# Attention loads in one queue, value products and transposes in other slots: a local-attention and gated-network kernel

## The chip, the cores and the metric

The kernel runs on one core of one Trainium2 chip. The metric is the device time of one execution in microseconds (us). The engines of a core are TensorE (PE in the profile: matrix products, with PEld for loading their stationary operand), VectorE (DVE), ScalarE (ACT), GpSimd (POOL) and SyncE (SP). Each engine works through its own list of instructions in order. DMAs (transfers between device memory and on-chip memory) are started from the lists of SyncE, ScalarE or GpSimd, and 16 DMA engines carry them out.

## What is computed

Local attention over chunks, then two gated networks, all in float32:

```python
# q, k, v: (4, 8, 768, 64); mem_k, mem_v: (4, 8, 8, 64)
for c in range(24):                                  # chunks of 32 queries
    l_start, r_end = max(0, 32*c - 16), min(768, 32*c + 40)
    k_full = concat([mem_k, k[:, :, l_start:r_end]])  # 8 memory keys + up to 56 keys
    v_full = concat([mem_v, v[:, :, l_start:r_end]])
    s = (q_c @ k_full.T) / 8
    a = exp(s - max(s));  a = a / (sum(a) + 1e-9)
    out_c = a @ v_full
x = out, as (3072 tokens, 512)
h = ((x @ w1) * (x @ w2)) @ w3;  x = h @ w_out        # 512 -> 1024 -> 512
y = ((x @ w_a) * (x @ w_b)) @ w_out2                  # 512 -> 1536 -> 512
```

## The kernel before, in words

The work is written out by hand in a set order; every engine's list follows the order of the program text.

**First stage.** The product of `w3` and `w_out` is formed on TensorE: two halves of 32 products of 128x512 outputs (in float32 each is two records `wps` in the trace), whose order is the list `order` of pairs (k, m). The weights arrive as raw blocks, `raw` (twelve of 1 MB: `w3a` x8, `w3b` x4; then sixteen of 0.5 MB of `w1`/`w2`), on SyncE's queue. `w_tick` moves a pipeline of four steps on by one: subtract the low part of one block, cast the high part of the next, sum the bits of the next on VectorE (`w_sum`, L359 and L360), scale the next on ScalarE (`w_scale`, L354 and L355), and then issue the loads whose buffers came free (`w_load`, L339; four buffers for the 1 MB blocks, three for the 0.5 MB ones). Three ticks run ahead of the first product, and 16 more among them.

**Attention.** The 3072 tokens are worked in 16 units of 192 tokens (u = 0 to 15). A unit loads its keys (`a_k`, two DMAs of 256 KB), queries (`a_q`, two of 192 KB) and values (`a_v`, twelve of 112 and 16 KB, as rows of 512 bytes); each of the three has one buffer, so the load of one unit waits until the unit before it has read that buffer. The steps of a unit are: `a_keys` (VectorE copies the key windows, L148, L149), `a_scores` (96 small matmuls `sc`), `a_max` (VectorE), four `a_exp` (ScalarE, four exponentials L195 each), two `a_norm` (sum and reciprocal on VectorE, the product on GpSimd, L212), `a_trans` (eight transposes `pt` on TensorE, L223), `a_pt` (ScalarE copies them out, L229), `a_pv` (96 small matmuls `xp` with the values) and `a_x` (the result is split into a high part on ScalarE and a low part on VectorE). `xp` and `pt` share one PSUM buffer.

**Slots.** `STAGES` gives each step its slot relative to 9u, and `attn_slot` runs all steps of one slot in the order of the table. In the first stage `attn_slot` is called after certain products; at its end the slots up to `NEED[0]` are done. In the second stage (the first network over six tiles of 512 tokens, `ti` = 0 to 5) the function `between`, called after each twelve large matmuls (`psA`, `psB`) or part of `psY`, does a `w_tick` while there are `w1`/`w2` blocks, later a step of converting the second network's weights (`cw`), and then as many slots as bring the count on evenly to `NEED[ti + 1]`: 27 or 18 slots in 22 calls. The third stage, from 621 us on, has no attention.

**Queues.** Loads of units 0 to 2 (`u < UA`) are issued from GpSimd, except the keys and queries of unit 0, which are issued from ScalarE after the third tick; from unit 3 on all are on SyncE. Weights, results and intermediate stores are on SyncE as well.

Of the kernel before, what the change touches and what calls it, by code (L numbers as in the profile page):

```python
# [14 lines left out]
B, H, S, D = 4, 8, 768, 64  # L15
NMEM = 8
CHUNK, LEFT, RIGHT = 32, 16, 8
GQ = 96
# [5 lines left out]
TT = 512  # L24
NT1 = B * S // TT
NU = B * NG * 2
NE = 2
NA = B * NG // NE
UA = -(-TT // (NE * GQ))
# [16 lines left out]
def tile_attention_moe(  # L46
# [16 lines left out]
    nc = tc.nc  # L63
# [25 lines left out]
    def mm(o, l, r, first, last):  # L89
        nc.tensor.matmul(o, lhsT=l, rhs=r, start=first, stop=last)  # L90
# [8 lines left out]
    def split_lo(lo, src, hi):  # L99
        nc.vector.tensor_tensor(lo, src, hi.bitcast(F32), ALU.subtract)  # L100

    def queue_of(u):
        return nc.gpsimd if u < UA else nc.sync

    def rows(r):
        return slice(D * r, D * r + D)

    def a_k(u, eng=None):
        if u >= NA:
            return  # L110
        k = ks[u] = att.tile([P, NE * 2, 2 * KW], F32, tag="kraw", bufs=1, name="kraw")
        for r in range(2):
            src = kt[2 * NE * u : 2 * NE * u + 2 * NE, 0:D, 2 * r : 2 * r + 2, :]
            (eng or queue_of(u)).dma_start(out=k[rows(r)], in_=src.rearrange("a d h k -> d a (h k)"))

    def a_q(u, eng=None):
        if u >= NA:
            return
        q = qs[u] = att.tile([P, NE * 2, 2 * GQ], F32, tag="q", bufs=1, name="q")
        for r in range(2):  # L120
            src = qt[2 * NE * u : 2 * NE * u + 2 * NE, :, 2 * r : 2 * r + 2, :]
            (eng or queue_of(u)).dma_start(out=q[rows(r)], in_=src.rearrange("a d h q -> d a (h q)"))

    def a_v(u):
        if u >= NA:
            return
        v = vs[u] = att.tile([P, NE * 2, NC, 2 * D], F32, tag="v", bufs=1, name="v")
        for r in range(2):
            src = vw[2 * NE * u : 2 * NE * u + 2 * NE, :, 2 * D * r : 2 * D * r + 2 * D]
            src = src.rearrange("a k d -> k a d")  # L130
            for c in range(NC):
                k0 = NMEM + CHUNK * c
                eng = queue_of(u)
                eng.dma_start(out=v[D * r : D * r + NMEM, :, c, :], in_=src[0:NMEM])  # L134
                eng.dma_start(  # L135
                    out=v[D * r + NMEM : D * r + D, :, c, :], in_=src[k0 : k0 + KEYS - NMEM]
                )

    def a_keys(u):
        if u >= NA:  # L140
            return
        k = ks.pop(u).rearrange("p a (h k) -> p (a h) k", h=2)
        kw = kws[u] = att.tile([P, NH, NC, KEYS], F32, tag="kw", bufs=1, name="kw")
        p, a, e = k.ap
        win = bass.AP(
            k.tensor, k.offset + NMEM * e[0], [p, a, [CHUNK * e[0], NC], [e[0], KEYS - NMEM]]
        )
        nc.vector.tensor_copy(kw[:, :, :, NMEM:], win)  # L148
        nc.vector.tensor_copy(  # L149
            kw[:, :, :, 0:NMEM], k[:, :, None, 0:NMEM].to_broadcast([P, NH, NC, NMEM])  # L150
        )
# [38 lines left out]
    def a_exp(i):  # L190
        def stage_of(u):
            sc, t, mx, sm = soft[u]
            for a in range(2 * i, 2 * i + 2):
                for r in range(2):
                    nc.scalar.activation(  # L195
                        t[:, a, r, :],
                        sc[:, r, a, :],
                        AF.Exp,
                        bias=mx[:, r, a : a + 1],
                        scale=SCALE,  # L200
                        accum_out=sm[:, a, r : r + 1],
                    )

        return stage_of

    def a_norm(e):
        def stage_of(u):
            t, mx, sm = soft[u][1:]
            t, sm = t[:, 4 * e : 4 * e + 4], sm[:, 4 * e : 4 * e + 4]
            nc.vector.tensor_scalar_add(sm, sm, 1e-9)  # L210
            nc.vector.reciprocal(sm, sm)
            nc.gpsimd.tensor_tensor(  # L212
                t, t, sm[:, :, :, None].to_broadcast([GQ, 4, 2, KEYS]), ALU.mult
            )

        return stage_of
# [33 lines left out]
    def a_x(u):  # L250
# [17 lines left out]

    NS_U = 9
    STAGES = (  # L270
        (10, a_x),
        (8, a_pt),
        (9, a_pv),
        (7, a_trans),
        (1, a_max),
        (2, a_exp(0)),
        (3, a_exp(1)),
        (3, a_exp(2)),
        (4, a_exp(3)),
        (4, a_norm(0)),  # L280
        (5, a_norm(1)),
        (0, a_scores),
        (1, lambda u: a_q(u + 1)),
        (5, lambda u: a_keys(u + 1)),
        (6, lambda u: a_k(u + 2)),
        (10, lambda u: a_v(u + 1)),
    )
    todo = {}
# [1 line left out]
        for j, (s, stage_of) in enumerate(STAGES):  # L290
            todo.setdefault(NS_U * u + s, []).append((j, u, stage_of))
    acount = [0]
    NEED = [NS_U * (-(-TT * (i + 1) // (NE * GQ)) - 1) + 11 for i in range(NT1)]

    def attn_slot(n=1):
        for _ in range(n):
            s = acount[0]
            if s >= NEED[-1]:
                return
            acount[0] += 1  # L300
            for _, u, stage_of in sorted(todo.get(s, []), key=lambda x: x[:2]):
                stage_of(u)
# [83 lines left out]
    def w_tick():  # L386

        if len(pipe[2]):
            i, a, ax, (d, f, w, hi, lo) = pipe[2].pop(0)
            nc.vector.tensor_tensor(lo, a, hi.bitcast(F32), ALU.subtract)  # L390
            live["dec"][ax] -= 1
            d[f] = w
        if pipe[1]:
            i, a, ax = pipe[1].pop(0)
            t = w_place(*plan[i][:3])
            nc.scalar.activation(t[3], a, AF.Copy)
            pipe[2].append((i, a, ax, t))
        if len(pipe[0]):
            i, r, tag = pipe[0].pop(0)
            a, ax = w_sum(i, r)  # L400
            live[tag][int(tag == "raw2")] -= 1
            if ax is not None:
                pipe[1].append((i, a, ax))
        if wraw:
            i, r, tag = wraw.pop(0)
            for (r1,) in pieces_of(i, r):
                w_scale(r1)
            pipe[0].append((i, r, tag))
        while w_load():
            pass  # L410
# [122 lines left out]
    w_load()  # L533
    for i in range(3):
        w_tick()
    a_k(0, nc.scalar)
    a_q(0, nc.scalar)

    def w_evict(half, m):
        w = wsm[4 * half + m] = w_new(wpool, "wo")  # L540
        nc.scalar.activation(w[:, 0, :], banks[m], AF.Copy)
        nc.vector.tensor_tensor(w[:, 1, :], banks[m], w[:, 0, :].bitcast(F32), ALU.subtract)
# [3 lines left out]
    for half in range(2):  # L546
        banks = [psd.tile([P, 512], F32, tag="d", name="wps") for _ in range(4)]
        for k, m in order:
            mm(
                banks[m],  # L550
                w3k[8 * half + k].bitcast(F32)[:, P * m : P * m + P],
                wo_f[k].bitcast(F32),
                k == 0,
                k == 7,
            )
            if k < 6 and m % 2 == 0 or k == 6:
                continue

            if half == 0:
                if k == 2 and m == 3:  # L560
                    a_keys(0)
                    a_k(1)
                    a_v(0)
                if m == 1 or k == 7 and m == 3:
                    w_tick()
                attn_slot(int(k > 2))
            else:
                if k < 6:
                    if m == 3:
                        w_tick()  # L570
                    attn_slot(1 + (m == 3 and k < 5))
                else:
                    if m % 2 == 1:
                        w_tick()
                    if m < 2:
                        attn_slot()
            if k == 7 and m > 0:
                w_evict(half, m - 1)
        w_evict(half, 3)
# [36 lines left out]
    def between():  # L616
# [10 lines left out]
        if ti < NT1 - 1:  # L627
            b = nstep[0] - NB * ti
            n = (NEED[ti + 1] - NEED[ti]) * b // (NB - 2)
            attn_slot(min(NEED[ti] + n, NEED[ti + 1]) - acount[0])  # L630

# [49 lines left out]
    for ti in range(NT1):  # L681
        last = ti == NT1 - 1
        gs = {}
        attn_slot(NEED[ti] - acount[0])
        if last:
# [320 lines left out]
```

## Time and profile before

| | |
|---|---|
| median of 3 runs | 1165.67 us (1165.38 to 1169.14) |
| the profiled execution | 1166.5 us; span 1164.7 us from its first to its last instruction, 1.8 us around it |
| TensorE busy | 1072.4 us (92% of the span) |
| VectorE, ScalarE, GpSimd busy | 462.9, 440.0, 264.8 us |
| mean granted clock of TensorE | 0.963 of 2.4 GHz (0.50 is 1.2 GHz) |
| first large matmul of the second stage | at 154.36 us |

A large matmul (128x512) is the unit in which TensorE works; a product of the first stage is two of them, a block of `psA` or `psB` twelve. A time in brackets behind an instruction is how long its engine stood idle before it, and the name behind the arrow is what ended that; "issue" means that the profile shows nothing the engine waited for.

### The profile page before, as it was taken

Reading aid. Unit: us, or ns where it says so; the run is one execution under the profiler, and the core shown is the slowest. Engines: PE = TensorE matmul, PEld = TensorE weight load, DVE = VectorE, ACT = ScalarE, POOL = GpSimd, SP = SyncE. Lnnn points to the kernel's source line nnn. Section 1 sums busy time; section 2 is a strip of 40 time slices with the busy share of each in tenths; the row PEclk is TensorE's granted clock in tenths of the full one; section 3 lists DMA queues with packets and bytes.
Section 4 is the critical chain, followed back from the end, with each engine's and each line's share of the span. In section 5 each row is a group of like instructions: output and inputs, shape, how many; then the busy total and the mean of one; then the engine's idle time right before and its main releaser. Section 6 shows DMA issues by size and latency. Waiting matters only on the chain.

```text
span 1164.7 us, 18629 instructions
## 1 busy us (share of the span) xinstructions
PE 1072.4 (92%) x7442; PEld 857.8 (74%) x7442; DVE 462.9 (40%) x763; ACT 440.0 (38%) x1153; POOL 264.8 (23%) x272
## 2 busy tenths in 40 slices
PE   6553489899999999999999999999999999999998
PEld 2222267787788778788888888888888888888887
DVE  3431267324445355253566334344222325222220
ACT  6332366444355365344444333333222223222220
POOL 0223212202122123031121322311232220323210
PEclk9777799899999999999999999999999999999999
DMA  9712544464345454632654554552444352534400
GB/s 338 218 54 66 131 132 124 131 186 132 110 150 154 147 157 138 184 108 102 221 193 157 199 207 171 208 174 74 160 151 166 127 199 73 189 128 143 174 37 36
DMA packets 80411, 173.22 MB, mean 149 GB/s; under 512 B 8317, under 2 KB 42621, under 8 KB 74437
## 3 DMA queue, kind: packets, MB, share of 16 engines
q1 hardware_dynamic: 66644, 100.82, 27.4%
q0 software_dynamic: 12384, 70.27, 16.9%
q8 instruction: 58, 0.95, 0.3%
q10 hardware_dynamic: 1296, 0.96, 0.3%
q14 instruction: 29, 0.23, 0.1%
HBM read 138.45 MB, written 33.55 MB: 148 GB/s over the span
## 4 chain that ended last, share of the span: by engine, by line
PE 80%; issue 9%; DMA 4%; POOL 3%; ACT 2%; DVE 1%; SPq 1%; POOLq 0%; ACTq 0%; DVEq 0%
PE ps L792 29%; PE ops L90 17%; PE psB L90 10%; PE psA L90 9%; PE psY L90 9%; PE xp L90 2%; DMA kraw<-in_kt 1%; PE sc L90 1%; PE wps L90 1%; POOL t L212 1%; POOL v L134 1%; POOL v L135 1%; DMA raw<-in_w3a 1%; PE pt L223 1%; ACT t L195 1%
## 5 line engine op out<-in xcount | busy, mean ns | idle before, releaser
L792 PE MATMUL ps<-x,w 128*128 128x512 f32 x1512 | 348.8, 389 | 0.3 <-ACT tmp L804 0.3
L792 PEld LDWEIGHTS ps<-x,w 128*128 128x128 f32 x1512 | 283.4, 188 | 60.3 <-ACT tmp L804 1.4
L809 DVE TENSOR_TENSOR tmp<-ps,tmp 128x512 f32<-128x512 f32 x108 | 74.6, 691 | 260.7 <-PE ps L792 230.9
L611 POOL TENSOR_TENSOR g<-gv,g 128x512 fp32r<-128x512 f32 x48 | 67.9, 1415 | 347.8 <-ACT g L610 319.5
L90 PE MATMUL psB<-xt,w 128*128 128x512 f32 x576 | 142.5, 397 | 0.0
L90 PE MATMUL psA<-xt,w 128*128 128x512 f32 x576 | 140.7, 393 | 0.0
L90 PE MATMUL psY<-g,wo 128*128 128x512 f32 x576 | 136.1, 395 | 0.0
L90 PEld LDWEIGHTS psB<-xt,w 128*128 128x128 f32 x576 | 109.5, 191 | 23.0
L90 PEld LDWEIGHTS psA<-xt,w 128*128 128x128 f32 x576 | 108.4, 189 | 23.5 <-issue 0.7
L90 PEld LDWEIGHTS psY<-g,wo 128*128 128x128 f32 x576 | 108.5, 190 | 22.9
L676 POOL DMA_DIRECT2D w<-wc x72 | 39.6, 552 | 373.7 <-PE ps L792 373.3
L804 ACT ACTIVATE tmp<-ps 128x512 f32<-128x512 f32 x108 | 64.4, 597 | 157.9 <-PE ps L792 147.3
L90 PE MATMUL ops<-wo,g 128*128 128x512 f32 x504 | 118.6, 389 | 0.0
L90 PEld LDWEIGHTS ops<-wo,g 128*128 128x128 f32 x504 | 94.6, 188 | 19.6
L815 ACT ACTIVATE g<-tmp 128x512 fp32r<-128x512 f32 x66 | 40.7, 633 | 139.9 <-DVE tmp L814 139.9
L816 POOL TENSOR_TENSOR g<-tmp,g 128x512 fp32r<-128x512 f32 x66 | 84.0, 1291 | 20.4 <-ACT g L815 19.4
L195 ACT ACTIVATE t<-sc,mx 96x64 f32<-96x64 f32 x256 | 75.3, 313 | 9.1 <-DVE mx L187 9.1
L223 PE MATMUL pt<-id_sb,t 96*128 96x96 f32 x128 | 16.7, 273 | 60.4 <-POOL t L212 60.1
L90 PE MATMUL ops<-fo,g 128*128 128x512 f32 x288 | 68.2, 389 | 0.0
L609 DVE TENSOR_TENSOR gv<-psB,av 128x512 f32<-128x512 f32 x48 | 33.1, 689 | 80.4 <-PE psB L90 66.6
L90 PE MATMUL wps<-w_f 128*128 128x512 f32 x128 | 62.6, 645 | 0.3 <-DVE w_f L360 0.2
L223 PEld LDWEIGHTS pt<-id_sb,t 96*128 96x128 f32 x128 | 13.6, 155 | 66.4 <-POOL t L212 65.0
(69 smaller groups left out, 1009.4 us busy)
## 6 DMA issues: line engine op xcount, KB each, us to landing
w<-wc POOLq DMA_DIRECT2D x36, 1024.0 KB, 6.8
w<-wc POOLq DMA_DIRECT2D x36, 768.0 KB, 4.9
wc<-co SPq DMA_DIRECT2D x84, 256.0 KB
raw<-in_wab SPq DMA_DIRECT2D x24, 512.0 KB
v<-in_vw SPq DMA_DIRECT2D x78, 112.0 KB
raw<-in_w SPq DMA_DIRECT2D x16, 512.0 KB
kraw<-in_kt SPq DMA_DIRECT2D x26, 256.0 KB
raw<-in_w3a SPq DMA_DIRECT2D x6, 1024.0 KB
```

Of the source, the lines that this page charges most:

```text
L90: nc.tensor.matmul(o, lhsT=l, rhs=r, start=first, stop=last)
L134: eng.dma_start(out=v[D * r : D * r + NMEM, :, c, :], in_=src[0:NMEM])
L195: nc.scalar.activation(t[:, a, r, :], sc[:, r, a, :], AF.Exp, bias=mx[:, r, a : a + 1], scale=SCALE, accum_out=sm[:, a, r : r + 1],)
L223: nc.tensor.transpose(pt[:, a // 4, a % 4, :], t[:, a].rearrange("p r k -> p (r k)"), id_sb)
L609: nc.vector.tensor_tensor(gv, psB[:, :TT], av, ALU.mult)
L611: nc.gpsimd.tensor_tensor(g2[:, 1, :], gv, g2[:, 0, :].bitcast(F32), ALU.subtract)
L676: nc.gpsimd.dma_start(out=t[:, c0:c1].bitcast(F32), in_=src[:, c0:c1])
L792: nc.tensor.matmul(ps, lhsT=w[:, i, a, k, :], rhs=xs[i][:, b, k, :], start=first and n == 0, stop=n == 5, skip_group_check=not first,)
L804: nc.scalar.activation(z, ps, AF.Copy)
L809: nc.vector.tensor_tensor(z, ps, y, ALU.add)
L815: nc.scalar.activation(g2[:, 0, :], z, AF.Copy)
L816: nc.gpsimd.tensor_tensor(g2[:, 1, :], z, g2[:, 0, :].bitcast(F32), ALU.subtract)
```

## The change

All attention loads are issued on SyncE's queue. Keys and queries of unit 0 are issued after the first of the three ticks that run ahead, so behind the first four weight blocks and ahead of the fifth. The values of unit 0 are issued at the product (k = 2, m = 1) and the keys of unit 1 still at (2, 3), behind the keys copy. The table of slots changes: `a_x` from 10 to 9, `a_pv` from 9 to 8, `a_pt` from 8 to 7, `a_trans` from 7 to 6, `a_norm` from 4 and 5 to 3 and 4, the exponentials from 2, 3, 3, 4 to 2, 2, 3, 3 (the first `a_norm` ahead of the third), the next unit's queries from 1 to 2, its keys copy from 5 to 7, the key load of the unit after it from 6 to 8. `a_pv` of a unit had the same slot as `a_scores` of the next (9), and now has the slot before it. `NEED` is one less throughout, and one slot less is run in the first stage's second half.

```diff
-    def queue_of(u):
-        return nc.gpsimd if u < UA else nc.sync
...
-    def a_k(u, eng=None):
+    def a_k(u):
...
-            (eng or queue_of(u)).dma_start(out=k[rows(r)], in_=src.rearrange("a d h k -> d a (h k)"))
-
-    def a_q(u, eng=None):
+            nc.sync.dma_start(out=k[rows(r)], in_=src.rearrange("a d h k -> d a (h k)"))
+
+    def a_q(u):
...
-            (eng or queue_of(u)).dma_start(out=q[rows(r)], in_=src.rearrange("a d h q -> d a (h q)"))
+            nc.sync.dma_start(out=q[rows(r)], in_=src.rearrange("a d h q -> d a (h q)"))
...
-                eng = queue_of(u)
-                eng.dma_start(out=v[D * r : D * r + NMEM, :, c, :], in_=src[0:NMEM])
-                eng.dma_start(
+                nc.sync.dma_start(out=v[D * r : D * r + NMEM, :, c, :], in_=src[0:NMEM])
+                nc.sync.dma_start(
...
-        (10, a_x),
-        (8, a_pt),
-        (9, a_pv),
-        (7, a_trans),
+        (9, a_x),
+        (7, a_pt),
+        (8, a_pv),
+        (6, a_trans),
         (1, a_max),
         (2, a_exp(0)),
-        (3, a_exp(1)),
+        (2, a_exp(1)),
+        (3, a_norm(0)),
         (3, a_exp(2)),
-        (4, a_exp(3)),
-        (4, a_norm(0)),
-        (5, a_norm(1)),
+        (3, a_exp(3)),
+        (4, a_norm(1)),
         (0, a_scores),
-        (1, lambda u: a_q(u + 1)),
-        (5, lambda u: a_keys(u + 1)),
-        (6, lambda u: a_k(u + 2)),
+        (2, lambda u: a_q(u + 1)),
+        (7, lambda u: a_keys(u + 1)),
+        (8, lambda u: a_k(u + 2)),
         (10, lambda u: a_v(u + 1)),
...
-    NEED = [NS_U * (-(-TT * (i + 1) // (NE * GQ)) - 1) + 11 for i in range(NT1)]
+    NEED = [NS_U * (-(-TT * (i + 1) // (NE * GQ)) - 1) + 10 for i in range(NT1)]
...
     for i in range(3):
         w_tick()
-    a_k(0, nc.scalar)
-    a_q(0, nc.scalar)
+        if i == 0:
+            a_k(0)
+            a_q(0)
...
             if half == 0:
+                if k == 2 and m == 1:
+                    a_v(0)
                 if k == 2 and m == 3:
                     a_keys(0)
                     a_k(1)
-                    a_v(0)
...
-                    attn_slot(1 + (m == 3 and k < 5))
+                    attn_slot(1 + (m == 3 and k < 4))
```

## Rows read from the trace of the kernel before

**Rows 1.** The page: TensorE's share and instructions; the instruction queue (packets, MB, share)

```profile
PE 1072.4 (92%) x7442; PEld 857.8 (74%) x7442; DVE 462.9 (40%) x763; ACT 440.0 (38%) x1153; POOL 264.8 (23%) x272
...
q8 instruction: 58, 0.95, 0.3%
```

**Rows 2.** Stretches: PE, PEld, DVE, ACT, POOL busy us, granted clock, DMA share, GB/s

```profile
12.00:15.00 3.00, 3.00 (x9) 1.25 (x7) 1.33 (x2) 2.33 (x3) 0.00 (x0) 1.00 1.02 431
54.00:69.00 15.00, 0.00 (x0) 0.00 (x0) 0.00 (x0) 0.00 (x0) 4.46 (x9) 0.50 0.17 47
0.00:154.40 154.40, 83.92 (x835) 41.28 (x835) 50.59 (x84) 60.87 (x158) 34.68 (x54) 0.78 0.51 157
154.40:621.00 466.60, 449.01 (x4235) 371.08 (x4234) 230.59 (x401) 225.00 (x735) 100.82 (x78) 0.98 0.48 151
```

**Rows 3.** TensorE's waits, 0 to 154 us: for what, us, times, longest

```profile
PE pt L223 <- POOL t L212: 55.4, 3, 22.9
PE sc L90 <- DMA q<-in_qt: 11.2, 2, 11.0
PE sc L90 <- issue: 1.8, 1, 1.8
```

**Rows 4.** TensorE in order of time: start, us, group [idle before, releaser]

```profile
70.70 1.90 PE L223 MATMUL pt<-id_sb,t 96*128 96x96 f32 x8 [22.86 <-POOL t L212]
...
81.55 8.85 PE L90 MATMUL wps<-w_f 128*128 128x512 f32 x20
...
160.22 2.88 PE L90 MATMUL psA<-xt,w 128*128 128x512 f32 x12
...
203.67 0.82 PE L223 MATMUL pt<-id_sb,t 96*128 96x96 f32 x8
```

**Rows 5.** GpSimd in order of time: its first load and its first normalisation

```profile
31.28 0.79 POOL L114 DMA_DIRECT2D kraw<-in_kt  x1 [30.84 <-DVE kw L149]
...
69.58 2.05 POOL L212 TENSOR_TENSOR t<-t,sm 96x512 f32<-96x512 f32 x2
```

**Rows 6.** Groups up to 155 us, by form: busy us, mean ns, idle before

```profile
L90 PE MATMUL wps<-w_f 128*128 128x512 f32 x128 | 62.6, 645 | 0.3 <-DVE w_f L360 0.2
...
L195 ACT ACTIVATE t<-sc,mx 96x64 f32<-96x64 f32 x48 | 14.1, 319 | 9.1 <-DVE mx L187 9.1
L360 DVE CUSTOM_DVE_ANT_0 w_f<-raw,w_f 128x2048 uint16<-128x2048 uint16 x10 | 12.3, 1226 | 1.6 <-ACT raw L355 1.1
L135 POOL DMA_DIRECT2D v<-in_vw x18 | 12.1, 671 | 48.2 <-issue 48.2
L354 ACT ACTIVATE raw<-raw 128x1024 f32<-128x1024 f32 x10 | 11.5, 1145 | 6.3 <-DMA raw<-in_w3a 6.3
...
L186 DVE TENSOR_REDUCE mx<-sc 96x16 f32<-96x1024 f32 x4 | 4.9, 1218 | 1.5 <-PE sc L90 1.4
```

**Rows 7.** Chain that ended last: the first weight blocks, the first keys

```profile
2.69 9.42 DMA raw<-in_w3a
...
12.87 16.97 DMA kraw<-in_kt
```

**Rows 8.** The SyncE queue in order of time: issues of query and value loads

```profile
149.61 1.26 SPq L122 DMA_DIRECT2D q<-in_qt  x2
...
151.56 0.33 SPq L135 DMA_DIRECT2D v<-in_vw  x1
```

**Rows 9.** TensorE in order of time after 154 us: three stalls

```profile
185.31 0.35 PE L90 MATMUL sc<-kw,q 64*32 64x64 f32 x13 [2.73 <-issue]
185.59 4.47 PE L90 MATMUL psB<-xt,w 128*128 128x512 f32 x12
...
211.02 2.96 PE L90 MATMUL xp<-p,v 64*64 64x32 f32 x96 [3.73 <-ACT p L229]
```

**Rows 10.** TensorE's waits, 240 to 640 us

```profile
PE sc L90 <- issue: 6.1, 4, 2.0
```

**Rows 11.** Waits of the SyncE queue over the whole span

```profile
SPq L114 <- DMA kraw<-in_kt: 37.3, 1, 37.3
```

## The prediction

> **What bounds the kernel now.** I read the page first: TensorE is busy 1072.4 us of 1164.7 [rows 1], so 92 us of idle time, and whatever it ran slowly, is all that a change of order can win. Then the table by stretch [rows 2]. The first stage (the combining products, up to 154.4 us) holds 83.9 us of TensorE work: 70.5 us idle, at a mean granted clock of 0.78. From 154.4 to 621 us it idles 17.6 us, and the tail after that about 4. So the first stage decides. Third, TensorE's waits there [rows 3]: 55.4 us in three waits before the transposes of units 0 to 2, all released by GpSimd's normalisation (L212); 11.2 us before the first scores, released by the query load; 1.8 us in the middle of a score block. In order of time the first of the three is 22.86 us long [rows 4]; the others are 17.6 and 15.0.
>
> Why is L212 late? GpSimd's own rows show it: it issues its first load at 31.28 and reaches the first L212 at 69.58, 38 us later [rows 5]. In between stand 16 issues (keys and queries of unit 1, twelve value loads of unit 0), and the softmax had long been done. An issue's recorded span is 0.67 us, but 18 of the value issues have 48.2 us of "issue" idle before them, 2.7 us each [rows 6]. The transfers are not the limit: from 54 to 69 us the DMA engines are 17% busy at 47 GB/s, TensorE and every other engine but GpSimd stand still, and the clock is down to 0.50, which is 1.2 GHz [rows 2].
>
> **Part 1: the loads leave GpSimd and ScalarE.** On the SyncE queue a value load is issued in 0.33 us and two query loads in 1.26 us [rows 8]: a unit's 16 issues cost 12 x 0.33 + 2 x 1.26 = 6.5 us of SyncE instead of the 38 of GpSimd, and nothing of the softmax stands behind them. What takes the place of the wait? I walk the new order, W0 to W11 being the 1.05 MB weight blocks.
> - Start. The third block lands at 12.1 us [rows 7]; at 431 GB/s [rows 2] the fourth is there at 14.9. Today the keys of unit 0 are issued on ScalarE's queue at that time and take 17 us [rows 7], sharing the engines with W4 to W8. Behind W3 on one queue, 0.92 MB of keys and queries takes 2.1 us at 431 GB/s and 4.1 at half that; I take 3.3, so 18.2. W4 then lands at 20.8, its scaling (1.15 us a pass) and summing (0.7 + 1.23) [rows 6] end at 24.3, and the keys copy, which stands behind that sum on VectorE, at 25.4. TensorE still stops at 21.1 (32.1 less 11.0), so the wait falls from 11.2 to about 4.5: **-6.7 us**.
> - Unit 0. The scores, still at half clock, end at 27.3; reduction (1.22 [rows 6]) and mask by 29.2. At 2.6 us a block (2.4 at 431 GB/s) W7 lands at 28.6, and ScalarE scales it before the exponentials; 16 of these take 4.7 us (0.32 each, overlapping), two normalisations 1.03 us each [rows 5, 6]. The second is done at about 37.3. TensorE's twelve products of 0.885 us [rows 4] take it to 37.9. Wait: 0 to 1 us.
> - Unit 1. Behind W7 come the values of unit 0 (0.79 MB in 512-byte pieces, 3.6 us at half rate), W8, the keys of unit 1 (36.6 us), W9, W10 and its queries (43.4); its scores stand at 46, so the first half ends near 47 (today 82). From there reduction, two weight ticks and exponentials end the normalisation at 55.6, where TensorE arrives after eight products at 54.1: wait 1.6. Unit 2 has ten products and waits about 0.8.
> - The three waits together are 3 instead of 55.4: **-52.4 us**.
> - Clock. 128 matmul records took 62.6 us [rows 6]; at the rate of the block at 81.55 (20 in 8.85 [rows 4]) they take 56.6. The three transpose groups take 1.90 instead of 0.82 [rows 4]. Together 9.2 us of half clock; I keep 3 of them for the wait that stays at 21 us: **-6**.
> - The 1.8 us inside a score block [rows 3] falls under part 2.
>
> Sum: the second stage starts at 154.4 - 6.7 - 52.4 - 6 - 1.8 = 87.5 us. Bounds: below, the stage's TensorE work at full clock, 83.9 - 9.2 = 74.7; above, if each of the three chains loses 5 us to late blocks, 103.
>
> By bytes the queue holds: the stage moves 157 GB/s over 154.4 us [rows 2], 24 MB; in 88 us that is 275 GB/s, against 431 with large blocks.
>
> Issuing is the limit here: 48.2 us of gaps on GpSimd [rows 6]. The Trainium skill ("Perfetto Trace Analysis", DMA Optimizations) speaks against the edit: where issuing is the limit, it may help to spread the issues over SyncE, ScalarE and GpSimd. By that rule the limit moves to SyncE with three units of 6.5 us, and the sum is 1108 (a rival below).
>
> **Part 2: value products a slot ahead of the scores.** Six of the 15 units show TensorE idle in the middle of the 96 score matmuls, on nothing the profile shows: 1.8 in the first stage, 2.73 at 185.3 [rows 9], and four of together 6.1 [rows 10]. Today 96 value products and 96 scores run back to back. The instruction queue moved 0.95 MB in 58 packets for 14,884 TensorE instructions [rows 1]: 257 instructions a packet, or 128 matmuls with their weight loads. A run of 192 crosses two packet ends about every second time, and the stop comes at the second. Apart by a block of twelve large matmuls (2.88 us at 160.22 [rows 4]), the next packet has that time to come. The block after a stop can be slow too: 4.47 us at 185.59 [rows 9], against 2.88 [rows 4]. The stalls past 154 us are 2.73 + 6.1 = 8.8, with two such blocks 12; three unit borders in the second stage still have both in one step, and keep 3: **-9 us**.
>
> The Trainium skill ("Runtime: NRT & Kernel Launch", Instruction fetch mechanics) calls the crossing of a 16 KiB instruction block mostly hidden. By that rule these stalls are no fetches, the -9 and the -1.8 go, and the sum is 1099.
>
> **Part 3: queries a slot, keys copy and key load two slots later; normalisation and transposes a slot sooner.** At 211 us TensorE waits 3.73 us for L229, which stands behind a scaling that waits for the first block of the second network; the 96 value products after it take 2.96 us [rows 9]. Half of that is the half clock's, and the scores after them lose about 1: 6 in all. That block's load now stands behind a key load on SyncE which waits for the keys copy; in the new order the key load comes after it, and it can go as soon as its buffer is free, some three steps sooner: **-6 us**. The key copy (1.1 us) is still two slots ahead of the scores, whose slot is 2.3 us (22 steps of 2.88 for 27 slots). In the second stage, scores and transposes stand at least five steps apart instead of six: 13.6 to 14.4 us, for reduction 1.4, exponentials 4.7, normalisation 1.5 and ScalarE's other work, 3 to 5: 11 to 13. The room is 1 to 3 us. A wait costs nothing while it has room; for late ones I add **+4**, between 0 and +38 (all 13 units late by 1.3 with 1.6 of clock).
>
> **Sum.** -6.7 - 52.4 - 6 - 1.8 - 9 - 6 + 4 = -77.9. The profiled execution took 1166.5 us (span 1164.7 and 1.8 around it); the median shown is 1165.7. 1166.5 - 77.9 = 1088.6; I say **1088**.
>
> **Rivals.**
> - *Weights become the wait.* Attention loads go ahead of W4, W8 and W9 on one queue, and ScalarE, which scales in order, makes exponentials and evictions wait. For: the first-stage DMA is full at the start (share 1.02 [rows 2]). Against: 275 GB/s are enough. With 5 us a unit and 3 of clock, 1106. Chance 0.12.
> - *SyncE's issuing becomes the limit.* For: twelve issues of values in a row are 4 us, more than a step. Against: SyncE issues while it would wait. Three units of 6.5 us in full: 1108. Chance 0.03.
> - *Transposes too early in the second stage.* The +4 becomes +38: 1122. Against: today's waits there are small. Chance 0.06.
> - *The stalls in the scores are no fetches* and stay where they are, or move. For: the profile gives them no releaser. Against: all six come late in the run of 192. 1099. Chance 0.11.
> - *The order on SyncE makes it slower.* A key, query or value load waits for its single buffer and holds every weight load behind it. SyncE has stood 37.3 us on one key load [rows 11]. It would take 78 us of such waits that reach TensorE, two of that size, to end above today's time; but that one was a wait for GpSimd's late work, which goes. 1175. Chance 0.03.
> - *The change doesn't do what it says:* GpSimd's issue gaps are only the shadow of slow value transfers, which SyncE has as well. Then the three waits stay at 15 us and more: 1140. The 17% DMA share speaks against it. Chance 0.04.
>
> The forecast (1076 to 1098) has the rest, 0.61. The range: below, the kept 3 + 3 + 3 + 4 us at nothing and the first wait 1.5 us shorter give 1074; above, the weights' case and half of the transposes' case are within 1112. A change under 0.3% (3.5 us) can't be told from none: faster 0.95, same 0.02, slower 0.03.
>
> **What would show it.** Right: no load on GpSimd before L676; first scores near 25 us; transposes of units 0 to 2 near 38, 56 and 72 us; first psA near 88; granted clock of the first stage above 0.9; score stalls on "issue" in at most three units. Wrong: ScalarE's L354 waiting on raw<-in_w3a for over 10 us, TensorE's wait for L212 over 10 us in all, or SyncE held by a value load while L354 waits.

## The result, and the profile after

The changed kernel takes 1087.22 us (median of 4 runs, 1085.66 to 1091.75) against 1165.61 for the kernel before in as many runs: ratio 0.9327, 95% interval 0.9292 to 0.9362. The forecast was 1088. The profiled execution took 1088.65 us with a span of 1086.9; the granted clock's mean is 0.991 (0.963 before).

Line numbers after stand four lower than before: the normalisation L212 is L208, the transposes L223 are L219, their copies L229 are L225, the scaling L354 is L350, the value loads L134 and L135 are L130 and L131.

From the page after, the lines that answer to [rows 1]:

```profile
PE 1063.5 (98%) x7442; PEld 851.3 (78%) x7442; DVE 453.3 (42%) x763; ACT 440.8 (41%) x1153; POOL 236.0 (22%) x228
...
q8 instruction: 59, 0.97, 0.4%
```

The same work, 44 instructions fewer on GpSimd, and TensorE idles 23 us where it idled 92. The stretches, as in [rows 2], cut where the second stage now begins:

```profile
0.00:91.40 91.40, 79.01 (x835) 39.38 (x835) 52.03 (x83) 61.00 (x158) 7.23 (x10) 0.94 0.85 257
91.40:543.00 451.60, 445.06 (x4234) 366.31 (x4233) 219.98 (x402) 225.68 (x735) 99.48 (x78) 0.99 0.51 158
```

The first stage is 91.4 us long instead of 154.4, at a mean granted clock of 0.94 instead of 0.78, with the DMA engines at 0.85 instead of 0.51; the second takes 451.6 us instead of 466.6. From there to the end it is 543.9 us, before 543.7: nothing changed there. TensorE's waits in the first stage after, which answer to [rows 3]:

```profile
PE sc L90 <- DVE kw L145: 5.7, 1, 5.7
PE xp L90 <- ACT p L225: 2.2, 1, 2.2
...
PE pt L219 <- POOL t L208: 0.9, 1, 0.9
PE wps L90 <- issue: 0.8, 1, 0.8
PE xp L90 <- DMA raw<-in_w: 0.5, 1, 0.5
PE sc L90 <- issue: 0.5, 1, 0.5
```

The waits for the normalisation fell from 55.4 us to 0.9. A new one stands second: 2.2 us ahead of the value products of unit 0. TensorE in order of time, after, against [rows 4]:

```profile
27.11 1.95 PE L90 MATMUL sc<-kw,q 64*32 64x64 f32 x96 [5.73 <-DVE kw L145]
...
39.99 0.83 PE L219 MATMUL pt<-id_sb,t 96*128 96x96 f32 x8
...
46.48 2.87 PE L90 MATMUL xp<-p,v 64*64 64x32 f32 x96 [2.20 <-ACT p L225]
...
60.66 0.50 PE L219 MATMUL pt<-id_sb,t 96*128 96x96 f32 x4
62.10 0.55 PE L219 MATMUL pt<-id_sb,t 96*128 96x96 f32 x4 [0.95 <-POOL t L208]
...
78.49 0.83 PE L219 MATMUL pt<-id_sb,t 96*128 96x96 f32 x8
...
91.38 3.33 PE L90 MATMUL psA<-xt,w 128*128 128x512 f32 x12
```

The prediction had 25, 38, 56, 72 and 88 for the scores, the three transposes and the second stage. The lag is 2 us for the scores and unit 0, about 5 to 6.5 us for units 1 and 2, and 3.4 us for the second stage.

### The profile page after: what moved, and what is told of

It reads as the page before. It is cut to its first block, busy times and chain, and to the rows that moved or that the text cites. A ratio compares the mean times of both kernels' runs of the same rounds, so it can differ in the third digit from the quotient of the medians.

```text
span 1086.9 us, 18651 instructions
## 1 busy us (share of the span) xinstructions
PE 1063.5 (98%) x7442; PEld 851.3 (78%) x7442; DVE 453.3 (42%) x763; ACT 440.8 (41%) x1153; POOL 236.0 (22%) x228
## 2 busy tenths in 40 slices
DMA packets 85575, 173.23 MB, mean 159 GB/s; under 512 B 7920, under 2 KB 48880, under 8 KB 79600
## 4 chain that ended last, share of the span: by engine, by line
PE 91%; DMA 4%; ACT 2%; DVE 1%; issue 1%; POOL 0%; SPq 0%; ACTq 0%
PE ps L790 31%; PE ops L90 18%; PE psY L90 12%; PE psB L90 12%; PE psA L90 12%; PE xp L90 3%; DMA raw<-in_w3a 2%; PE sc L90 2%; PE wps L90 1%; ACT t L191 1%; DMA raw<-in_w 1%; DMA raw<-in_w3b 1%; PE pt L219 1%; ACT raw L351 0%; DMA id_sb<-in_ident 0%
## 5 line engine op out<-in xcount | busy, mean ns | idle before, releaser
L814 POOL TENSOR_TENSOR g<-tmp,g 128x512 fp32r<-128x512 f32 x66 | 84.0, 1291 | 20.8 <-ACT g L813 19.8
L90 PEld LDWEIGHTS ops<-fo,g 128*128 128x128 f32 x288 | 54.1, 188 | 11.2
L608 ACT ACTIVATE g<-gv 128x512 fp32r<-128x512 f32 x48 | 30.5, 636 | 74.5 <-DVE gv L607 74.4
L90 PE MATMUL wps<-w_f 128*128 128x512 f32 x128 | 59.4, 612 | 1.1 <-issue 0.8
```

The source lines that it names most:

```text
L608: nc.scalar.activation(g2[:, 0, :], gv, AF.Copy)
L814: nc.gpsimd.tensor_tensor(g2[:, 1, :], z, g2[:, 0, :].bitcast(F32), ALU.subtract)
```

## The experiments

The theory: the first stage's gain comes from the loads leaving GpSimd's list, where the normalisation stood behind them; the second stage's comes from the slots, through stalls at the ends of instruction packets that 192 small matmuls in a row bring out, and through the second network's first load. Its rivals: the value transfers themselves are slow and GpSimd's gaps only their shadow; the stalls belong to the data or to certain units and not to the list; what is left of the first stage is a matter of order. Two kernels take the change apart, three test the stalls, the rest the loads. Each is timed against the kernel before on the same chip. Beside these groups of runs the kernel before had medians of 1163.7 to 1165.6 us, so a difference from after of 1 to 2 us is not told from none.

**The queue alone.** After, with the slots, `NEED` and the slot count of before:

```diff
-        (9, a_x), (7, a_pt), (8, a_pv), (6, a_trans), ...
+        (10, a_x), (8, a_pt), (9, a_pv), (7, a_trans), ...   # all STAGES as before
-    NEED = [... + 10 ...]
+    NEED = [... + 11 ...]
-                    attn_slot(1 + (m == 3 and k < 4))
+                    attn_slot(1 + (m == 3 and k < 5))
```

> The changed kernel with the slot table, NEED and slot count of before: only the queue and the places of the first loads are new. Theory (the first stage is won by the loads leaving GpSimd, the second by the slots): first psA near 92 us instead of 154.4, TensorE's waits for the GpSimd normalisation in the first stage under 6 us instead of 55.4; the second stage as long as before (466 us, stalls inside the scores about 8 us), so about 1103 us (1098 to 1108). Rival (the slots do most of it): first psA above 120 us, 1135 or more.

1103.75 us, ratio 0.9482 (0.9467 to 0.9498). First `psA` at 94.34 us, the third stage at 559.32.

**The slots alone.** Before, with the slots of after:

```diff
-        (10, a_x), (8, a_pt), (9, a_pv), (7, a_trans), ...
+        (9, a_x), (7, a_pt), (8, a_pv), (6, a_trans), ...    # all STAGES as after
-    NEED = [... + 11 ...]
+    NEED = [... + 10 ...]
```

> The kernel before with the new slot table, NEED and slot count; the loads stay on GpSimd and ScalarE. Theory: GpSimd's issues still stand ahead of the normalisation, the three waits of TensorE stay at 50 us or more in all, first psA at 150 to 156; the second stage is 10 to 15 us shorter: 1152 us (1148 to 1158). Rival (normalisation a slot sooner gets ahead of the loads and does most of it): the waits halve, 1130 or less.

1150.78 us, ratio 0.9893 (0.9869 to 0.9916). First `psA` at 155.88, the third stage at 604.57. TensorE's waits of the slots-only kernel, first stage and second:

```profile
PE pt L223 <- POOL t L212: 56.9, 3, 24.3
...
PE sc L90 <- issue: 3.6, 2, 2.0
PE pt L223 <- POOL t L212: 0.9, 2, 0.7
PE xp L90 <- ACT p L229: 0.7, 1, 0.7
```

and of the queue-only kernel in its second stage:

```profile
PE sc L90 <- issue: 10.4, 6, 3.4
PE pt L219 <- POOL t L208: 3.6, 2, 2.5
PE xp L90 <- ACT p L225: 3.4, 2, 2.9
```

The two parts split the stages in the main. The queue takes 60.0 us from the first stage and 1.6 from the second; the slots take 17.9 from the second and add 1.5 to the first. They do not simply add up by stage: together they take 63.0 us from the first, 4.5 more than the sum of the two, and 15.0 from the second, 4.5 less. The slots alone leave the three long waits where they were; the queue alone leaves the score stalls, the transposes' waits and the wait for the second network's first block.

**Value products back with the scores.** After, with only `a_pv` and `a_x` in the slots of before:

```diff
-        (9, a_x),
+        (10, a_x),
-        (8, a_pv),
+        (9, a_pv),
```

(`NEED` and the slot count go with them.)

> The changed kernel with the value products (and a_x) back in the slot of the next unit's scores, everything else as changed. Theory (instruction blocks of 128 matmuls run out inside a run of 192 small ones): 5 to 8 of the 15 units stall on issue inside the scores, 1.3 to 2.7 us each, 10 us in all instead of 4.8, so 1093 us (1089 to 1098). Rival (the stalls have nothing to do with the two runs being adjacent): as many stalls as in the changed kernel, 1087 (1085 to 1089).

1097.05 us, ratio 0.9434 (0.9410 to 0.9459): 9.8 us slower than after. Seven units stall in the scores, 15.8 us in all; three of them, TensorE in order of time:

```profile
53.53 0.67 PE L90 MATMUL sc<-kw,q 64*32 64x64 f32 x23 [3.97 <-issue]
...
145.64 0.71 PE L90 MATMUL sc<-kw,q 64*32 64x64 f32 x47 [1.72 <-issue]
...
330.19 0.44 PE L90 MATMUL sc<-kw,q 64*32 64x64 f32 x22 [2.23 <-issue]
```

With 192 small matmuls in a row the stalls come back; besides the split of the result (`a_x`), nothing else of the order was changed.

**TensorE's list shifted.** If the stalls are ends of instruction packets, they must move when the list is shifted. In the trace of before they stand at the records 347, 1105, 1991, 2372, 3258 and 4144 of TensorE's matmuls: apart by 6, 7, 3, 7 and 7 times 126.3 to 127.0. TensorE's list also holds a weight load for each matmul and some instructions that wait for semaphores (the counters by which engines and loads signal to each other). Counted with these from the trace's records, the six stand at 704, 2240, 4032, 4800, 6592 and 8384 instructions, exactly 6, 7, 3, 7 and 7 times 256 apart.

The trace also has the packets of the instruction queue, q8, 16,384 bytes each. In the 13 traces TensorE stops 54 times for "issue" by 0.3 us or more; every stop is a whole number of 256 instructions from these places, to one or two instructions, and TensorE goes on 1.2 to 1.7 us after the end of one of these packets. For the stall of 2.73 us in [rows 9], the packet runs from 182.73 to 183.75, and the scores go on at 185.31. The kernel after with net 46 more tiny records ahead of all products:

```diff
-    for _ in range(5):
+    for _ in range(4):
         mm(warm[:GQ], wz[:, :GQ], wz, True, True)
+    for _ in range(SHIFT):                             # SHIFT = 24
+        mm(warm[:32, :64], wz[:, :32], wz[:, :64], True, True)
```

> The changed kernel with one warm-up matmul (two records) taken away and 48 small records added at the start, so that every later TensorE instruction stands 46 records further on; 0.3 us of work. Theory (a stall wherever two ends of instruction blocks, some 126.5 matmuls apart, fall in one run of small matmuls): unit 6's scores, which now don't stall, stall at their matmul 80 to 92 by 1.3 to 2.3 us; units 10's and 13's, which now stall at matmuls 73 and 69 by 1.7 and 1.8 us, stall no more or by under 0.9 us; the scores of unit 2 in the first stage stall near matmul 55. Time the same within 3 us. Rival (the stalls belong to the data, the DMA traffic or the unit): units 10 and 13 stall as now and unit 6 does not.

1092.23 us (1088.26 to 1096.19), ratio 0.9393 (0.9369 to 0.9416). TensorE in order of time:

```profile
72.08 1.07 PE L91 MATMUL sc<-kw,q 64*32 64x64 f32 x41 [3.61 <-issue]
...
172.59 0.32 PE L91 MATMUL sc<-kw,q 64*32 64x64 f32 x9 [1.63 <-issue]
...
322.51 0.92 PE L91 MATMUL sc<-kw,q 64*32 64x64 f32 x69 [0.32 <-issue]
```

The unit at 172 us, which had no stall, now has one of 1.63 us; that at 322 us keeps 0.32 of its 1.73, and the one at 400 us has none instead of 1.83. Data, loads and slots are the same. The shift also puts packet ends into the scores of units 2 and 3 in the first stage, where they cost 3.6 and 1.3 us: in the trace the first stage takes 96.4 us, 5.0 more than after, and the second 446.2, 5.4 less. So the profiled execution is as long as that of after (1088.26 and 1088.65 us). The median is 5 us longer, where the same time was expected; what lengthened the other three executions no trace shows.

**No unit border back to back.** After, three units of the second stage (two of them stalled) still have their value products and the next unit's scores in one step, because 27 slots go into 22 calls. Another rounding moves the doubled steps:

```diff
-            n = (NEED[ti + 1] - NEED[ti]) * b // (NB - 2)
+            n = ((NEED[ti + 1] - NEED[ti]) * b + 5) // (NB - 2)
```

> The changed kernel with the slots of the second stage rounded otherwise (5 added ahead of the division by 22), so that no step of it holds a unit's value products and the next unit's scores together. Theory (instruction blocks): the stalls of units 10 and 13 (1.73 and 1.83 us) and what follows them go, no other above 0.9 us comes; 1083 (1081 to 1086). Rival: stalls of the same size at other units, 1087.

1083.77 us, ratio 0.9310 (0.9282 to 0.9337), 3.5 us under the median of after, though the intervals overlap. In the second stage one stall is left, 0.94 us instead of 4.4 in three, and the stage takes 446.9 us instead of 451.6. Not all of these 4.7 us are the rounding's: three kernels below with the second stage of after (keys first, values later, values on ScalarE) take 449.2 to 449.7 us for it, with two stalls of 3.4 to 3.9 us together.

**The normalisation on VectorE.** Before, with the product of L212 off the engine whose list holds the issues:

```diff
-            nc.gpsimd.tensor_tensor(
+            nc.vector.tensor_tensor(
                 t, t, sm[...].to_broadcast(...), ALU.mult
```

> The kernel before, with the product of the normalisation on VectorE instead of GpSimd, so that nothing of the softmax stands behind GpSimd's load issues. Theory (twelve value issues of 2.7 us each are late themselves, and the value products need what they bring): TensorE's waits for L212 in the first stage are gone, but it waits for the value loads instead, 10 to 15 us a unit; the first psA at 135 to 150 us, 1148 to 1163 us. Rival (only the place of the normalisation behind the issues costs): the wait goes and none takes its place, first psA below 110, about 1115.

1150.60 us, ratio 0.9884 (0.9850 to 0.9918). TensorE's longest wait of the first stage is now

```profile
PE xp L90 <- DMA v<-in_vw: 41.1, 11, 8.8
```

So the normalisation's place in GpSimd's list was not the whole cost: with the product moved, the values themselves come late, since GpSimd stands 1.7 to 5.8 us ahead of every second value issue, as before [rows 6], and the first stage still takes 143.7 us. The trace of before shows what these gaps are: up to 76 us each ends 0.30 to 0.34 us after the landing of the larger load before it on GpSimd's queue, and the larger value loads land 2.6 to 7.1 us after their issue. So the gaps are the shadow of transfers, as the rival says, but of transfers that GpSimd starts one after the other; on SyncE, where several are under way at once, the same loads can be issued 0.37 us apart [rows 8], and the queue alone wins 60.0 us. The gain needed the loads off GpSimd's queue.

**Values on ScalarE's queue.** After, with the value loads of units 0 to 2 spread to a second queue:

```diff
-                nc.sync.dma_start(out=v[...], in_=src[0:NMEM])
+                (nc.scalar if u < UA else nc.sync).dma_start(out=v[...], in_=src[0:NMEM])
```

(The second load of each pair likewise.)

> The changed kernel with the value loads of units 0 to 2 issued on ScalarE's queue, all else on SyncE. Theory (what holds an issue is its place in line on a full DMA queue, and it holds what stands behind it on the issuing engine): ScalarE's scaling and exponentials of the first stage come 5 to 12 us later per unit, first psA at 100 us or later, 1095 to 1115 us. Rival (spreading the issues relieves SyncE and costs ScalarE nothing that shows): 1085 or less.

1108.26 us, ratio 0.9515 (0.9488 to 0.9542): 21 us slower than after. ScalarE's own work waits behind the issues, which stand in its list; from its timeline:

```profile
22.81 0.52 ACTq L130 DMA_DIRECT2D v<-in_vw  x1
...
32.51 0.49 ACTq L131 DMA_DIRECT2D v<-in_vw  x1
33.05 1.14 ACT L350 ACTIVATE raw<-raw 128x1024 f32<-128x1024 f32 x1 [8.16 <-DMA v<-in_vw]
```

ScalarE stands 8.16 us ahead of its next scaling, until the last value load is issued, and TensorE waits 14.7 us in six waits for the normalisation. SyncE isn't relieved either: it stands 10.0 us for the landing of a value load and issues its next weight block at 30.69 us. The Trainium skill ("Perfetto Trace Analysis", DMA Optimizations) says that spreading issues over the queues may help where issuing limits; here the queue it would spread to belongs to an engine that is needed, and the loads of both queues wait for each other (the reason stands with the new wait in the next section).

**Keys copied first.** The largest wait left, 5.7 us ahead of the first scores, is for the keys copy, which stands behind a block's sum on VectorE. After, with the copy ahead of that tick:

```diff
                 if k == 2 and m == 1:
                     a_v(0)
+                    a_keys(0)
                 if k == 2 and m == 3:              # behind the tick of (2, 1)
-                    a_keys(0)
                     a_k(1)
```

> The changed kernel with the keys copy of unit 0 ahead of the weight tick at (2, 1) instead of behind it; the loads stay. Theory (the 5.7 us wait before the first scores is the copy standing behind the sum of the fifth block on VectorE, but the blocks after it land no sooner): the wait falls to 0 to 2 us, and most of it comes back before block 4 and block 7 are summed; first psA 0 to 3 us sooner, 1084 to 1088. Rival (the wait is for the key load itself): it stays at 5 us or more.

1091.13 us, ratio 0.9373 (0.9340 to 0.9406): not faster. The wait is gone and stands at the products instead:

```profile
PE wps L90 <- DVE w_f L356: 6.7, 2, 5.1
```

The order on VectorE only decides which of TensorE's instructions waits.

**Values issued later.** After, with unit 0's values one tick later:

```diff
-                if k == 2 and m == 1:
-                    a_v(0)
...
+                if k == 3 and m == 1:              # behind the tick
+                    a_v(0)
```

> The changed kernel with the value loads of unit 0 issued behind the tick at (3, 1), so behind the issues of blocks 8 and 9 and the keys of unit 1. Theory (twelve value issues held SyncE from 19.7 to 33.0 us, block 8 was issued at 33.0 instead of 26, ScalarE waited for it and block 9 and made the value products of unit 0 wait 2.2 us): blocks 8 and 9 land sooner, that wait falls below 1 us, 2 to 4 us are won, 1083 to 1086. Rival (the hold only moves to block 10 and the queries of unit 1, or the values are late): 1087 or more.

1086.32 us, ratio 0.9331 (0.9310 to 0.9352): the same as after. The next weight block is issued at 26.05 us instead of 33.04, but the value issues now stretch from 29.34 to 41.8 and hold the block behind them until 41.84. The hold moves and hardly shrinks. TensorE's wait ahead of unit 0's value products is gone; instead it waits 1.0 us for the queries of unit 1 and stalls 1.7 us in those scores.

**Values in one load.** After, with the values laid out by the host in the order of the tile (memory keys and window of each chunk, repeated as the tile repeats them), so that a unit's twelve loads become one of the same bytes, in rows of 6 KB:

```diff
-        for r in range(2):
-            ...
-            for c in range(NC):
-                nc.sync.dma_start(out=v[... NMEM rows, :, c, :], in_=src[0:NMEM])
-                nc.sync.dma_start(out=v[... D - NMEM rows, :, c, :], in_=src[k0 : k0 + KEYS - NMEM])
+        nc.sync.dma_start(out=v.rearrange("p a c d -> p (a c d)"), in_=vw[u])
```

> The changed kernel with the values of a unit laid out by the host in the order of the tile, the same bytes on the chip: one load of 128 rows of 6 KB instead of twelve with rows of 512 bytes. Theory (SyncE is held 12 to 13 us by the many small pieces of a value load while the DMA engines are full): the issue takes under 1.5 us, block 8 is issued by 27 us instead of 33, the 2.2 us wait before unit 0's value products goes, first psA 2 to 5 us sooner, 1080 to 1085 us. Rival (SyncE is held by the bytes in front of it): block 8 is issued at 31 us or later, 1086 to 1088.

1077.74 us (1076.99 to 1077.78), ratio 0.9250 (0.9229 to 0.9272): 9.5 us faster than after, more than expected. The SyncE queue in order of time, and the two stretches:

```profile
19.62 0.42 SPq L125 DMA_DIRECT2D v<-in_vw  x1
25.93 0.33 SPq L327 DMA_DIRECT2D raw<-in_w3b  x1
```

```profile
0.00:88.40 88.40, 78.79 (x833) 0.94 0.87 266
88.40:531.90 443.50, 441.20 (x4235) 1.00 0.51 161
```

The second stage begins 2.9 us sooner and is 8.1 us shorter. The latter was not foreseen: in it one stall of 0.48 us is left (about 2 of the 8.1 us also separate after from the other kernels with its second stage). The three back-to-back borders are still there. The two stalls of this trace stand 2038 records apart, 16 packets of 127.4 instead of 126.0 to 126.4 after, and at that spacing the ends that hit the scores of two units after fall 6 and 10 records past their last one. The reason is in TensorE's list: with one load to wait for instead of twelve it has 92 semaphore instructions instead of 172, so more matmuls go into each 256 instructions.

**One load and the other rounding together**, with one slot of the first stage ahead of its tick as well:

```diff
+                first = k == 7 and m == 1
+                attn_slot(int(first))              # ahead of the tick
                 if m == 1 or k == 7 and m == 3:
                     w_tick()
-                attn_slot(int(k > 2))
+                attn_slot(int(k > 2 and not first))
```

> The changed kernel with three edits: the value loads in one piece, the other rounding of the second stage's slots, and in the first half the slot of (7, 1) ahead of its weight tick, so that the copy of the transposes of unit 0 doesn't stand behind the scaling of block 9. Theory: 3.5 us of stalls in the second stage and 3 to 5 us of the first go: 1079 us (1076 to 1082). Rival (the first stage is bound by the blocks' landing, whatever is moved): 1083.

1077.39 us (1077.03 to 1077.80), ratio 0.9248 (0.9226 to 0.9270). It equals the one load alone, in whose second stage hardly a stall was left to take away; in the first stage the wait for L225 is gone, but the stall in unit 1's scores is 2.7 us instead of 2.1. These two are the fastest versions tried.

## Why the prediction was right, step by step

**First stage: -66.9 predicted, -63.0 measured** (154.36 to 91.38).

- *Three waits for L212: -52.4 predicted, -54.5 measured* (55.4 to 0.9). The reason given, that the normalisation stood behind sixteen issues on GpSimd, holds: GpSimd has ten instructions in the first stage after, and unit 0's normalisations run at 35.70 and 38.53 us. The normalisation on VectorE adds a second cost of those issues, the late values, of which the sum had not spoken. That the transfers are not the limit holds for the DMA engines' share (17%), but not for the single load: each of GpSimd's gaps ended with the landing of a load before it.
- *First scores: -6.7 predicted, -5.5 measured.* W4 was forecast to land at 20.8; ScalarE waits for it until 22.72, and the scores start at 27.11 instead of 25.4, while TensorE stops at 21.38 (21.1 forecast). Part of the lag was in the working: from 12.1 the fourth block at 431 GB/s is there at 14.5, not 14.9, and ScalarE had it at 15.85.
- *Clock: -6 predicted.* TensorE's busy time in the stage fell by 4.9 us for the same 835 matmuls (83.92 to 79.01).
- *A new wait, not in the sum: +2.2* ahead of unit 0's value products. This is the rival in which the weights become the wait, in its mildest form, and the sign named for it, SyncE held by value loads while the scaling waits, is there. The mis-sized price is "a value load is issued in 0.33 us": the row behind it [rows 8] was read at 151 us, where the loads eight before had long landed. The SyncE queue after, in order of time, and its waits for loads from 19 to 34 us:

```profile
19.71 0.37 SPq L130 DMA_DIRECT2D v<-in_vw  x1
...
20.87 0.32 SPq L131 DMA_DIRECT2D v<-in_vw  x1
22.65 0.27 SPq L130 DMA_DIRECT2D v<-in_vw  x1
25.14 0.32 SPq L131 DMA_DIRECT2D v<-in_vw  x1
27.62 0.27 SPq L130 DMA_DIRECT2D v<-in_vw  x1
30.50 0.32 SPq L131 DMA_DIRECT2D v<-in_vw  x1
30.86 1.00 SPq L130 DMA_DIRECT2D v<-in_vw  x1
...
32.63 0.32 SPq L131 DMA_DIRECT2D v<-in_vw  x1
33.04 0.36 SPq L335 DMA_DIRECT2D raw<-in_w3b  x1
```

```profile
SPq L131 <- DMA raw<-in_w3a: 4.8, 2, 2.6
SPq L130 <- DMA raw<-in_w3a: 3.6, 2, 2.1
```

Each issue is short, but the fifth to the eighth stand 1.8 to 2.9 us apart; the twelve take from 19.71 to 33.04, 13.3 us where 4 were counted. What holds these four is the landing of the weight blocks W4 to W7: by the trace these land at 22.63, 25.13, 27.61 and 30.48, and the issues go 0.01 to 0.02 us later. The reason is in the program and not in the pieces: the loads of SyncE and ScalarE signal their landing on eight semaphores in turn, and a load is issued only when the one before it on its semaphore, here eight loads earlier, has landed. Twelve loads in a row therefore have to wait for what was issued ahead of them; four would not have. The weight block behind them goes out at 33.04, and ScalarE, in order, waits for it and the next:

```profile
38.80 1.15 ACT L350 ACTIVATE raw<-raw 128x1024 f32<-128x1024 f32 x1 [1.37 <-DMA raw<-in_w3b]
...
43.62 1.12 ACT L350 ACTIVATE raw<-raw 128x1024 f32<-128x1024 f32 x1 [2.59 <-DMA raw<-in_w3b]
...
45.63 0.79 ACT L225 ACTIVATE p<-pt 128x768 f32<-128x768 f32 x1
```

The transposes' copy L225 stands behind that scaling, and TensorE behind the copy. The one load of 6 KB rows agrees: the same bytes take one turn of the eight, and the next block goes out at 25.93. With the values issued later, the fifth to eighth value issues likewise go 0.01 to 0.02 us after the landing of the load eight before (33.43 to 39.59), and so do the sixth to the tenth on ScalarE's queue (25.18 to 31.26). So the hold hangs on the number of loads; what the 512-byte rows cost besides was not separated.

How much the hold costs TensorE is less sure than the hold itself. The kernel with the other rounding has the same first stage; there the wait is 0.6 us and the stall in the scores of unit 1 1.9 (after: 2.2 and 0.5), and unit 0's value products start at 46.4 and 46.5 in the two.

- *The stall in the first stage: -1.8 predicted, -0.5 measured*: 1.8 us became 0.5 in scores and 0.8 in a product.

**Second stage: -11 predicted (-9 -6 +4), -15.0 measured** (466.6 to 451.6).

- *Score stalls: -9.* Stalls of 8.8 us in five became 4.4 in three, two of them at the borders still back to back and 0.8 at one that is twelve large matmuls apart, so that distance doesn't always suffice; TensorE's busy time, with the slow blocks after stalls and waits, fell by 4.0 (449.01 to 445.06). The prediction kept 3 us for three such borders; the third has a packet end early in its scores and does not stall. Its count was off too: at most three units with a stall were named, and there are four, 0.46 us in the first of them. That the ends of packets stop TensorE is shown by the shifted list, by the back-to-back order, and by the stops' places, whole multiples of 256 instructions apart, and the packets that land ahead of TensorE's going on; the 257 instructions a packet worked out from [rows 1] came close.

The Trainium skill ("Runtime: NRT & Kernel Launch", Instruction fetch mechanics) has the same block of 256 instructions and calls its crossing mostly hidden. Among large matmuls it mostly is, in these traces (the longest stop there is 1.9 us, with the keys copied first); in runs of small ones the stops that showed are 0.3 to 4.4 us.

- *The second network's first block: -6.* The wait of 3.73 us ahead of the value products [rows 9] is gone: waits for L225 in the second stage fell from 4.0 to 1.5, with the slots alone to 0.7 and with the queue alone only to 3.4. So it is the slots' doing. Of these the key load's was the reason given; the first `in_wab` load is issued 36.5 us into the second stage after and 48.3 us into it before, which agrees, but that slot was not changed by itself. The 1.5 us left are a new wait, at unit 3; that at unit 4 is gone.
- *Later transposes: +4 predicted, -4.0 measured* (waits for the normalisation 4.7 to 0.7). This is the step with the wrong sign. The prediction priced the room between scores and transposes, which shrank from six steps to five, and put nothing on the other side for exponentials and normalisation that start a slot sooner. With the slots alone the waits are 0.9, with the queue alone 3.6: the gain is the slots', and which of the moves brings it was not taken apart.

The four parts, -4.4 in stalls, -2.5 in waits for L225, -4.0 in waits for the normalisation and -4.0 in busy time, make up the 15.0. TensorE's waits after, in the second stage:

```profile
PE sc L90 <- issue: 4.4, 3, 1.8
PE xp L90 <- ACT p L225: 1.5, 1, 1.5
PE pt L219 <- POOL t L208: 0.7, 1, 0.7
```

The first stage lost 4 us against the forecast and the second won 4, so the total of -77.9 came out at -77.9 (1166.5 to 1088.65) with terms that were off by as much. That it fits so closely is luck: the two errors have nothing to do with each other. The mechanisms of the two large terms, the loads on GpSimd and the packet ends, were right. One sign named as wrong proved useless: ScalarE's wait for `raw<-in_w3a` over 10 us is 11.1 after, but 8.9 of that stood there before.

Of the rivals, transposes too early, stalls that are no fetches, and a change that leaves the three waits are excluded by these numbers. SyncE's issuing did become a wait, worth the 2.4 to 2.9 us by which one load of the values shortens the first stage (88.4 us, against 90.9 and 91.4 in the two kernels with twelve and the same list), not 20.

## What to carry to other kernels

When compute waits on an engine that issues loads, count every issue in that engine's list between the data's arrival and the instruction, at the gap between issues and not at the length of one; and look for what ends each gap. Here it was the landing of the load eight before, on two queues together, so many small loads behind large ones hold whatever stands behind them, and a layout that makes them one load was worth more than another queue. Keep long runs of small matmuls apart by large ones: the next 256 instructions of the list have to arrive too.

## What was not expected of the hardware

- How many loads are issued matters as much as how many bytes: twelve loads took 13.3 us to issue among weight blocks, the same bytes in one load 0.42 us. That hold is the program's, by its eight semaphores. Over the whole kernel the packets fell from 85575 to 61189 for 173.2 MB in both. The Trainium skill ("Perfetto Trace Analysis", DMA Optimizations) says that DMAs under 2 KB have a large overhead each and that larger ones help. The 9.5 us agree with it, but how much of them is the longer rows' was not separated.
- The stalls in the scores are of very different length: 0.3 to 4.4 us over all traces, while the packet that ends each takes 0.9 to 1.6 us. What differs is when it starts: up to 2.8 us before TensorE stops, and in the five stops over 3 us 1.0 to 2.0 us after; TensorE goes on 2.3 to 3.1 us behind the start, whatever the length of the stop. These five packets take 0.9 to 1.1 us, so it isn't a slow transfer that makes the stops long. The DMA engines' share is 0.87 to 1.06 in about 3 us ahead of them, but 1.08 ahead of the one of 2.73 us too; what sets the start was not determined.
- The spacing of packet ends in recorded matmuls is not fixed at 128: 126.0 to 126.4 after and 127.4 with the one load, since semaphore instructions take places too. It decides which unit stalls, and so a few microseconds, in kernels whose work is otherwise the same.
